# Attention and a maxout feed-forward layer: weight loads by column groups and six-tile groups of Q and K in place of whole-expert loads and per-tile loads, with another order

## The chip, the cores and the metric

The kernel runs on one core of a Trainium2 chip. The core has five engines with a queue each: TensorE (PE; its weight loads are listed as PEld), VectorE (DVE), ScalarE (ACT), GpSimd (POOL) and SyncE (SP), which here issues nearly all DMA transfers. The metric is the device time of one execution in microseconds (us). The kernel before took 182.6, 183.34 and 183.36 us in three runs; the median is 183.34 us.

## The reference

Input are q, k and v of four batches, eight heads, 768 positions and 64 elements a head, in fp32, and four weight matrices. First comes attention with a window: a query sees the keys at most 95 positions behind it, and the first eight keys of its batch.

```python
scores = scale * np.matmul(q, k.transpose(0, 1, 3, 2))
rel = pos[:, None] - pos[None, :]
is_global = pos[None, :] < int(n_global)             # 8
is_local = (rel >= 0) & (rel < int(n_local))         # 96
keep = is_global | is_local
dist = np.where(is_global & ~is_local, float(n_local), np.abs(rel))
scores = scores - slopes[:, None, None] * dist       # one slope a head
scores = np.where(keep, scores, -1000000000.0)
a = softmax(scores)
x = (a @ v), heads put side by side                  # 3072 x 512
```

Then comes a feed-forward layer with three experts, of which the largest value counts:

```python
h = np.maximum(np.maximum(x @ w1, x @ w2), x @ w3)   # 3072 x 768
return (h @ w_out).astype(np.float32)                # 3072 x 512
```

## The kernel before, in words

The 3072 positions are 24 tiles of 128, six to a batch. The whole program is one list of units, SCHEDULE (lines 25 to 57), written out by a planner and executed from left to right (lines 474 and 475). A unit is a letter and numbers; each issues its instructions to the engines' queues, and each engine works through its queue in this order. Waits between engines follow from the data and from the buffers. The letters (line 471):

- `l n.s` loads part s of group n of Q or K (line 151), `c n.s.how` casts it to bf16 (line 178), and `x n.s.how` transposes it on TensorE and copies it from PSUM to the transposed Q and K of the batch, qkT (line 226). A group is several tiles of a batch (GROUPS, line 91: first tile and number). A row of the load holds as many positions of a head as the group has tiles, so it is 256 bytes times that number. Groups of 2 tiles have two parts (Q and K, all heads), groups of 4 four parts, groups of 6 eight parts (two heads each).
- `L T` loads one tile of Q and K in rows of 256 bytes (line 160), `C T.0.how` casts it and `X T.how` transposes it, on TensorE or, with how 4, by a DMA transpose from SP's queue (line 245). `v T` loads V and `C T.1.how` casts it.
- `S T.g.how` computes the scores of four heads of a tile (g is 0 or 1) and their exponential on ACT (line 268). With how 1 TensorE adds the bias with two further matmuls; with how 0 a later unit `M T.g` multiplies by a mask on VectorE (line 302). `B` and `K` prepare the biases and masks.
- `A T.how` is the product with V and the division by the sum (line 311; how names which of two PSUM buffers it takes). `G` and `V` put the first eight keys and values of the batch into the tile, in place of its own (lines 209 and 218), once the tile's own are no longer needed.
- `T T.how` transposes the attention's result, on TensorE or (how 4) by DMA (line 335), into xT of a chunk. There are seven chunks, of 4, 2, 2, 4, 4, 4 and 4 tiles.
- `w g.j` loads weights of expert j (line 412), `W g.j.how` casts column group g of expert j (256 of 768 columns; line 425), `o` and `Q` do the same for w_out.
- `F c.f.j` computes 128 hidden columns f of chunk c for expert j with four matmuls (line 355). Expert 0's result is copied by ACT to a buffer h01, and VectorE takes the maximum with the other two.
- `O c.t.how` is one tile of the output: six matmuls, a copy and a store (line 385); `E` does the last chunk's (line 390).

In casts and copies how is 0 for ACT, 1 for VectorE and 2 for POOL. For `x`, how 0 and 1 transpose into the single PSUM buffer psT and copy on ACT and VectorE, 2 and 3 do so in the three buffers psH, which the `F` and `O` units use too, and 4 splits the copy between ACT and VectorE.

Buffers that matter: raw (6) for loads of Q and K, cast_pool (5), h01 (6), psH (3), psT (1), the two score buffers of PSUM sp0 and sp1 (1 each), and three stages for weights of 1.5 MB (line 414).

Of the kernel before, what the change touches and what calls it, by code (L numbers as in the profile page):

```python
# [12 lines left out]
FP32 = mybir.dt.float32  # L13
# [9 lines left out]


SCHEDULE = """
    B0.1 B1.1 B2.1 B3.1 v0 B4.2 l1.0 l1.1 K0 K1 K2 K3 K4 K5 K6 K7 B5.0 c0.0.2 c0.1.1 B6.1 x0.0.2 B7.1
    x0.1.4 v1 S0.0.1 S0.1.1 G0.2 S1.0.1 c1.0.2 x1.0.3 v2 M0.0 M0.1 S1.1.1 M1.0 C0.1.2 M1.1 A0.0 c1.1.2
    C1.1.2 l2.0 l2.1 x1.1.4 C2.1.0 A1.1 V1.1 c2.0.1 G1.0 T0.1 S2.0.1 T1.1 S2.1.0 G2.2 S3.0.1 S3.1.1 G3.0
    M2.0 M2.1 v3 C3.1.1 w0.0 M3.0 M3.1 A2.0 w0.1 v4 v5 w0.2 x2.0.2 l3.0 l3.2 V2.2 A3.1 T2.1 c2.1.2
    x2.1.4 T3.0 W0.0.1 S4.0.0 S4.1.1 F0.0.0 G4.2 S5.0.0 S5.1.0 W1.0.2 V3.1 F0.1.0 F0.2.0 W2.0.2 F0.3.0  # L30
    F0.4.0 F0.5.0 W1.1.0 l3.1 l3.3 M4.0 M4.1 W2.1.0 W0.2.2 v6 v7 C4.1.1 W0.1.1 M5.0 M5.1 C5.1.0 W1.2.0
    c3.0.2 A4.1 c3.2.2 F0.0.1 F0.1.1 F0.2.1 V4.1 F0.3.1 F0.4.1 F0.5.1 c3.1.2 c3.3.2 A5.0 T4.0 F0.0.2
    x3.0.2 W2.2.0 o2 o1 F0.1.2 F0.2.2 Q1.2 l4.0 T5.1 o0 x3.2.2 F0.3.2 x3.1.1 F1.0.0 F1.1.0 C6.1.1 x3.3.2
    F1.2.0 F0.4.2 S6.0.0 S6.1.0 G6.0 M6.0 M6.1 F0.5.2 S7.0.0 S7.1.0 G7.2 l4.1 F1.0.1 F1.0.2 F1.1.1
    F1.1.2 F1.3.0 A6.1 F1.2.1 F1.3.1 S8.0.0 S8.1.0 F1.2.2 F1.3.2 Q2.2 c4.0.2 C7.1.2 M7.0 M7.1 F1.4.0
    G8.2 F1.5.0 S9.0.0 S9.1.0 G9.2 F1.4.1 F1.5.1 F1.4.2 M8.0 v8 L12 L13 v9 Q0.0 c4.1.2 F1.5.2 v10 A7.0
    C8.1.0 x4.0.4 x4.1.2 O0.0.0 T6.0 M8.1 M9.0 V7.2 C12.0.1 O0.1.0 S10.0.0 L14 S10.1.0 G10.2 v11 M9.1
    M10.0 O0.2.1 X12.4 T7.1 O0.3.1 A8.0 C13.0.0 C9.1.0 V8.2 T8.4 F2.0.0 F2.1.0 F2.2.0 A9.1 X13.1 V9.2
    C14.0.0 v12 C10.1.2 F2.0.1 F2.1.1 F2.2.1 S11.0.0 S11.1.0 F2.3.0 F2.4.0 M10.1 M11.0 O1.0.0 X14.0
    M11.1 A10.1 V10.2 F2.0.2 F2.1.2 F2.2.2 T9.1 C11.1.0 S12.0.0 S12.1.0 G12.0 F2.3.1 F2.4.1 S13.0.0  # L40
    S13.1.0 F2.3.2 T10.0 F2.5.0 F2.4.2 A11.0 G13.2 M12.0 L15 L16 v13 v14 O1.1.1 F2.5.1 C12.1.0 T11.0
    S14.0.0 S14.1.0 G14.2 F2.5.2 M12.1 M13.0 M13.1 M14.0 M14.1 C13.1.1 C15.0.2 F3.0.0 F3.1.0 F3.2.0
    X15.4 C16.0.1 X16.4 A12.1 T12.4 F3.3.0 F3.4.0 v15 A13.0 L17 L18 v16 L19 F3.0.1 F3.1.1 F3.2.1 S15.0.0
    S15.1.0 G15.2 M15.0 O2.0.0 M15.1 F3.0.2 F3.1.2 C14.1.0 V13.2 A14.1 O2.1.0 S16.0.0 M16.0 S16.1.0
    G16.1 F3.3.1 F3.2.2 F3.3.2 C15.1.2 C17.0.0 V14.2 A15.1 T13.4 T14.4 T15.4 C18.0.2 X17.0 F3.4.1 F3.5.0
    V15.2 M16.1 C16.1.1 C19.0.2 S17.0.0 S17.1.0 F3.4.2 F3.5.1 F3.5.2 A16.0 X18.4 V16.2 v17 v18 M17.0
    X19.1 O3.0.0 O3.1.0 O3.2.0 C17.1.2 F4.0.0 F4.0.1 S18.0.0 S18.1.0 F4.0.2 G18.0 F4.1.0 v19 S19.0.0
    S19.1.0 F4.2.0 F4.3.0 L20 C20.0.2 T16.4 G19.1 M17.1 L21 M18.0 M18.1 M19.0 C18.1.2 F4.4.0 F4.1.1
    F4.5.0 M19.1 F4.2.1 F4.3.1 X20.4 A17.1 F4.1.2 C19.1.1 F4.4.1 F4.5.1 A18.0 A19.1 F4.2.2 F4.3.2 F4.4.2
    T17.4 S20.0.0 S20.1.0 F4.5.2 T18.4 T19.4 L22 O3.3.1 F5.0.0 C21.0.1 X21.4 C22.0.0 G20.2 F5.0.1 M20.0  # L50
    M20.1 F5.1.0 F5.2.0 X22.4 F5.1.1 F5.3.0 F5.4.0 S21.0.0 S21.1.0 F5.2.1 F5.3.1 F5.4.1 M21.0 G21.0
    S22.0.0 v20 L23 v21 v22 S22.1.0 F5.0.2 M21.1 M22.0 F5.5.0 F5.5.1 M22.1 C20.1.2 V19.2 A20.0 V20.2
    F5.1.2 F5.2.2 F5.3.2 C21.1.0 v23 A21.0 C23.0.0 X23.4 T20.4 T21.4 O4.0.1 V21.2 C22.1.2 A22.1 C23.1.1
    V22.2 O4.1.1 G22.2 F5.4.2 T22.4 S23.0.0 M23.0 S23.1.0 F5.5.2 O4.2.0 O4.3.0 M23.1 A23.1 T23.4 O5.0.1
    O5.1.1 O5.2.0 O5.3.0 F6.0.0 F6.1.0 F6.2.0 F6.0.1 F6.1.1 F6.3.0 F6.2.1 F6.3.1 F6.4.0 F6.0.2 F6.1.2
    F6.2.2 F6.5.0 F6.4.1 F6.3.2 F6.4.2 F6.5.1 F6.5.2 E
"""


# [1 line left out]
def kernel(  # L61
# [13 lines left out]
    nc = tc.nc  # L75
# [8 lines left out]
    DM = H * D  # L84
    DFF = moe_w1.shape[1]
# [2 lines left out]
    slopes = [2.0 ** (-8.0 * (h + 1) / H) for h in range(H)]  # L88
    sizes = [4, 2, 2, 4, 4, 4, 4]

    GROUPS = [[0, 2], [2, 2], [4, 2], [6, 4], [10, 2]]
    assert sum(sizes) == NTT
    chunks, where = [], {}
    for n in sizes:
# [15 lines left out]
    xT_pool = ctx.enter_context(tc.tile_pool(name="xT", bufs=3))  # L110
    stage_pool = ctx.enter_context(tc.tile_pool(name="stage", bufs=3))
    ht_pool = ctx.enter_context(tc.tile_pool(name="ht", bufs=2))
    h01_pool = ctx.enter_context(tc.tile_pool(name="h01", bufs=6))
    ost_pool = ctx.enter_context(tc.tile_pool(name="ost", bufs=4))
    psS = ctx.enter_context(tc.tile_pool(name="psS", bufs=1, space=bass.MemoryType.PSUM))
    psH = ctx.enter_context(tc.tile_pool(name="psH", bufs=3, space=bass.MemoryType.PSUM))
# [14 lines left out]
    w123 = [persist.tile([128, 4, 3, 256], BF16, name=f"w123_{i}") for i in range(3)]  # L131
# [12 lines left out]
    def part(n, s):  # L144

        T0, sz = GROUPS[n]
        jn = {2: 4, 4: 2, 6: 1}[sz]
# [3 lines left out]
    def load_part(n, s):  # L151

        bb, t0, sz, a, j0, jn = part(n, s)
        r = raw_pool.tile([128, 2 * DM], FP32, name="rawp", tag="raw")
        r = r[:, 0:sz * jn * 128].rearrange("i (h x) -> i h x", h=2 * jn)
        raw["p", n, s] = r
        src = (q, k)[a][bb, 2 * j0:2 * (j0 + jn), t0 * 128:(t0 + sz) * 128, :]
        nc.sync.dma_start(out=r, in_=src.rearrange("h (i e) d -> i h (e d)", e=sz))  # L158
# [17 lines left out]
    copies = (nc.scalar.copy, nc.vector.tensor_copy, nc.gpsimd.tensor_copy)  # L176
# [231 lines left out]
    wsrc = [moe_w1, moe_w2, moe_w3]  # L408

    wst = {}  # L410

    def load_w(g, j):

        st = stage_pool.tile([128, 4, DFF], FP32, name="wst", tag="wst")
        wst[j] = st
        nc.sync.dma_start(out=st, in_=wsrc[j].rearrange("(i p) f -> p i f", p=128))

    def load_wo(i):
        st = stage_pool.tile([128, 4, DFF], FP32, name="wost", tag="wst")
        st = st.rearrange("p i f -> p (i f)")[:, 0:2 * DM].rearrange("p (i f) -> p i f", i=2)  # L420
        wst["o", i] = st
        nc.sync.dma_start(out=st, in_=moe_w_out[i * 256:(i + 1) * 256, :].rearrange(
            "(i p) f -> p i f", p=128))

    def cast_w(g, j, how):
        copies[how](w123[g][:, :, j], wst[j][:, :, 256 * g:256 * (g + 1)])  # L426

    def cast_wo(i, how):
        copies[how](wo[:, 2 * i:2 * i + 2], wst["o", i])
# [7 lines left out]
    with tc.manual_schedule():  # L437
        load_part(0, 0)
        load_part(0, {2: 1, 4: 2, 6: 4}[GROUPS[0][1]])

# [6 lines left out]
        for tvar in va_ring + va_first:  # L447
# [21 lines left out]
        nc.vector.tensor_scalar_min(rbase[0:NG, 2, :], rbase[0:NG, 2, :], float(NL))  # L469

        units = {"l": load_part, "v": load_v, "c": cast_part, "x": u_x, "L": load, "w": load_w, "o": load_wo, "C": cast, "X": u_X, "S": u_S, "M": u_M,
                 "A": u_A, "G": put_kg, "V": put_vg, "T": u_XT, "F": u_F1, "W": cast_w,
                 "K": u_K, "B": u_B, "Q": cast_wo, "O": u_F2, "E": u_E, "D": u_D}
        for u in SCHEDULE.split():
# [34 lines left out]
```

The softmax here doesn't subtract the row's maximum and nothing guards it: scores larger than these inputs give would overflow.

## Time and profile before

The profiled execution took 182.6 us, and the profile's span is 180.8 us; the rest lies around it.

| engine | busy us | share of the span | instructions |
|---|---|---|---|
| PE | 166.4 | 92% | 1532 |
| PEld | 95.1 | 53% | 1552 |
| DVE | 119.1 | 66% | 233 |
| ACT | 104.5 | 58% | 159 |
| POOL | 38.0 | 21% | 66 |

The page divides the span in 40 slices of 4.52 us and gives each engine's busy share in tenths. A chain of waits is followed back from the last instruction; each line of it has a start, a duration and the work ("PE h L361 x47": 47 matmuls of line 361 in a row; "SPq": SP issuing a DMA; "DMA wst": a transfer). A timeline has start, duration, engine, line, operation and, in brackets, the idle time ahead of it and what ended it. A group has its count, busy time and mean duration. The time to landing of a DMA counts from its issue on SP. DMA queue q1, which SP's transfers use, moved 35.2 MB.

### The profile page before, as it was taken

The page shows a single profiled execution, that of the slowest core. Times are in us where ns is not written, and L with a number is a line of the kernel's source. Part 1 is how long each engine was busy: PE and PEld are TensorE (multiplying, and loading weights), DVE is VectorE, ACT ScalarE, POOL GpSimd, SP SyncE. Part 2 cuts the span into 40 slices and gives each one's busy share as a digit, 9 for nine tenths or more (in the row PEclk, how much of TensorE's full clock was granted, in tenths as well). Part 3 has the DMA queues.
Part 4 walks back from the last instruction along what each step waited for, and adds up shares of the span by engine and source line. Part 5 has one row for each costly group of instructions (what it writes and reads, how often), then busy time and mean ns, then how long its engine had stood idle before and what let it go on. Part 6 is the DMA issues. An engine that isn't in the chain of part 4 may idle for free.

```text
span 180.8 us, 3975 instructions
## 1 busy us (share of the span) xinstructions
PE 166.4 (92%) x1532; PEld 95.1 (53%) x1552; DVE 119.1 (66%) x233; ACT 104.5 (58%) x159; POOL 38.0 (21%) x66
## 2 busy tenths in 40 slices
PE   0598879999999999999999999999999999999990
PEld 0344635466777587755455544554445545444450
DVE  4538755986789787689758816597739984046600
ACT  4958878756779868974656358304566242421141
POOL 6470370261551020020123310400004300000000
PEclk9999999999999999999999999999999999999997
DMA  5999999999979798975599999925899664600024
GB/s 145 271 252 282 387 359 247 378 316 322 321 169 219 202 184 238 225 196 93 124 220 252 151 264 248 154 58 110 186 153 218 126 167 151 232 0 4 0 79 155
DMA packets 82035, 35.52 MB, mean 196 GB/s; under 512 B 66144, under 2 KB 76768, under 8 KB 82016
## 3 DMA queue, kind: packets, MB, share of 16 engines
q1 hardware_dynamic: 81872, 35.20, 84.5%
q8 instruction: 12, 0.20, 0.5%
q10 hardware_dynamic: 144, 0.07, 0.1%
q14 instruction: 7, 0.06, 0.1%
HBM read 25.17 MB, written 6.29 MB: 174 GB/s over the span
## 4 chain that ended last, share of the span: by engine, by line
PE 82%; SPq 7%; DMA 7%; issue 1%; ACT 1%; DVE 0%; ACTq 0%
PE h L361 52%; PE po L376 16%; DMA wst<-in_moe_w_dram 6%; PE sp L283 5%; SPq L158 4%; SPq L174 3%; PE op L322 3%; PE op L325 2%; PE tpp L239 1%; DMA out_dram<-ost 1%; PE tp L261 1%; PE xtp L349 1%; DVE w L426 0%; ACT P L288 0%; ACT ost L382 0%
## 5 line engine op out<-in xcount | busy, mean ns | idle before, releaser
L361 PE MATMUL h<-xT,w 128*128 128x512 bf16 (+1 forms) x491 | 99.0, 348 | 1.9 <-DVE w L426 1.1
L361 PEld LDWEIGHTS <-w 128*128 128x128 bf16 x504 | 46.9, 98 | 41.8 <-DVE w L426 1.3
L288 ACT ACTIVATE P<-sp 128x1024 bf16<-128x1024 f32 (+1 forms) x48 | 43.4, 953 | 24.2 <-PE sp L283 24.2
L368 DVE TENSOR_TENSOR h<-h,h 128x512 bf16<-128x512 bf16 (+1 forms) x42 | 25.1, 608 | 20.3 <-PE h L361 17.1
L376 PE MATMUL po<-wo,ht 128*128 128x512 bf16 (+2 forms) x149 | 33.2, 362 | 0.4
L366 ACT CAST h<-h 128x512 bf16<-128x512 f32 (+1 forms) x42 | 21.4, 533 | 17.7 <-PE h L361 17.4
L370 DVE TENSOR_TENSOR ht<-h,h 128x512 bf16<-128x512 bf16 (+1 forms) x42 | 24.9, 608 | 8.7 <-PE h L361 8.0
L307 DVE TENSOR_TENSOR P<-P,wmask 128x1024 bf16<-128x1024 bf16 x34 | 22.9, 693 | 5.1 <-ACT P L288 5.1
L376 PEld LDWEIGHTS <-ht 128*128 128x128 bf16 x156 | 14.2, 98 | 14.0
L382 ACT COPY ost<-po 128x512 f32<-128x512 f32 (+2 forms) x17 | 9.3, 556 | 20.5 <-PE po L376 19.0
L332 DVE TENSOR_TENSOR xb<-op,rz 128x512 bf16<-128x512 f32 x24 | 16.6, 691 | 0.8
L283 PEld LDWEIGHTS <-qkT 64*128 64x128 bf16 x352 | 10.1, 95 | 10.9 <-issue 8.0
L283 PE MATMUL sp<-qkT 64*128 64x128 bf16 x352 | 15.5, 221 | 0.1
L239 PE MATMUL tpp<-identb,qkp 128*128 128x128 bf16 x96 | 8.0, 234 | 6.7 <-POOL qkp L183 6.4
L322 PEld LDWEIGHTS <-P 128*128 128x128 bf16 x192 | 12.5, 97 | 2.8 <-ACT P L288 0.5
L322 PE MATMUL op<-va,P 128*128 128x65 bf16 x160 | 12.5, 193 | 0.6 <-ACT P L288 0.6
L325 PEld LDWEIGHTS <-P 128*128 128x128 bf16 x160 | 10.4, 97 | 1.7 <-issue 0.2
L183 POOL CAST qkp<-rawp 128x1024 bf16<-128x1024 f32 x10 | 10.5, 1052 | 2.3 <-DMA rawp<-in_k_dram 1.2
L239 PEld LDWEIGHTS <-qkp 128*128 128x128 bf16 x96 | 6.4, 105 | 7.8 <-POOL qkp L183 6.7
L382 DVE COPY ost<-po 128x512 f32<-128x512 f32 (+1 forms) x9 | 5.8, 643 | 6.4 <-PE po L376 6.4
L325 PE MATMUL op<-va,P 128*128 128x65 bf16 x128 | 9.9, 193 | 0.1
L221 POOL COPY va<-vaf 8x260 int32<-8x260 int32 x13 | 5.6, 430 | 20.5 <-PE op L325 14.5
(64 smaller groups left out, 111.7 us busy)
## 6 DMA issues: line engine op xcount, KB each, us to landing
rawv<-in_v_dram SPq DMA_DIRECT2D x24, 256.0 KB, 5.2
out_dram<-ost SPq DMA_DIRECT2D x23, 256.0 KB, 2.3
wst<-in_moe_w_dram SPq DMA_DIRECT2D x3, 1536.0 KB, 10.3
rawp<-in_q_dram SPq DMA_DIRECT2D x6, 512.0 KB, 7.3
rawp<-in_k_dram SPq DMA_DIRECT2D x6, 512.0 KB, 7.9
raw<-in_q_dram SPq DMA_DIRECT2D x12, 256.0 KB, 4.9
raw<-in_k_dram SPq DMA_DIRECT2D x12, 256.0 KB, 5.1
wost<-in_moe_w_out_dram SPq DMA_DIRECT2D x3, 512.0 KB, 6.9
```

Source lines behind the costliest of these rows:

```text
L239: nc.tensor.transpose(tp[:, e, j - lo], qb["p", n, s][:, e, 2 * j:2 * j + 2].rearrange("i h d -> i (h d)"), identb)
L283: nc.tensor.matmul(sp[:, hh, j2, ds], qT(T - ds, 1)[hsl, jp], qT(T, 0)[hsl, jp], start=not how, stop=True, skip_group_check=True)
L288: nc.scalar.activation(P[:, :, 0:n], sp.rearrange("p a b d n -> p (a b) d n")[:, :, 0:n], AF.Exp, bias=0.0, scale=scale)
L307: nc.vector.tensor_mul(P, P, wmask[:, g, :, 0:2])
L322: nc.tensor.matmul(o, P[:, i, 0], heads(va[T])[:, h], start=True, stop=(t == 0), skip_group_check=True)
L325: nc.tensor.matmul(o, P[:, i, 1], heads(va[T - 1])[:, h], start=False, stop=True, skip_group_check=True)
L332: nc.vector.tensor_tensor(out=x.rearrange("p (g h) d -> p g h d", g=2), in0=o4[:, :, :, 0:64], in1=rz[:, :, :, None].to_broadcast([128, 2, ...
L361: nc.tensor.matmul(ps, w123[f // 2][:, dm, j, (f % 2) * 128:(f % 2) * 128 + 128], xT[c][:, dm], start=(dm == 0), stop=(dm == 3))
L366: nc.scalar.copy(h01, ps)
L368: nc.vector.tensor_max(h01s[c, f], h01s[c, f], ps)
L370: nc.vector.tensor_max(ht[c][:, f], h01s[c, f], ps)
L376: nc.tensor.matmul(po, ht[c][:, f, tt * 128:(tt + 1) * 128], wo[:, f, cols], start=(f == 0), stop=(f == NF - 1))
```

## The change

There are four parts.

1. GROUPS: the fourth group is tiles 6 to 11 (all of batch 1) in place of tiles 6 to 9, the fifth is tiles 12 to 17 (all of batch 2) in place of tiles 10 and 11. Both have eight parts of 128 rows for two heads, 1536 bytes a row. Tiles 12 to 17 have no `L`, `C T.0` and `X` units any longer; tiles 18 to 23 keep them.
2. Each expert's weights come in two loads: columns 0 to 255 (0.5 MB, rows of 1024 bytes; `w0.j`) and columns 256 to 767 (1 MB, rows of 2048 bytes; `w1.j`). They have stages of their own, three each; w_out takes the first kind.
3. h01 has four buffers in place of six.
4. The list is planned anew.

```diff
-    GROUPS = [[0, 2], [2, 2], [4, 2], [6, 4], [10, 2]]
+    GROUPS = [[0, 2], [2, 2], [4, 2], [6, 6], [12, 6]]
...
-    h01_pool = ctx.enter_context(tc.tile_pool(name="h01", bufs=6))
+    h01_pool = ctx.enter_context(tc.tile_pool(name="h01", bufs=4))
...
     def load_w(g, j):
-        st = stage_pool.tile([128, 4, DFF], FP32, name="wst", tag="wst")
-        wst[j] = st
-        nc.sync.dma_start(out=st, in_=wsrc[j].rearrange("(i p) f -> p i f", p=128))
+        n = 256 * (1 + g)
+        st = stage_pool.tile([128, 4, n], FP32, name="wst", tag=f"wst{g}")
+        wst[g, j] = st
+        nc.sync.dma_start(out=st, in_=wsrc[j][:, 256 * g:256 * g + n].rearrange("(i p) f -> p i f", p=128))
 
     def load_wo(i):
-        st = stage_pool.tile([128, 4, DFF], FP32, name="wost", tag="wst")
-        st = st.rearrange("p i f -> p (i f)")[:, 0:2 * DM].rearrange("p (i f) -> p i f", i=2)
+        st = stage_pool.tile([128, 2, DM], FP32, name="wost", tag="wst0")
...
     def cast_w(g, j, how):
-        copies[how](w123[g][:, :, j], wst[j][:, :, 256 * g:256 * (g + 1)])
+        src = wst[0, j] if g == 0 else wst[1, j][:, :, 256 * (g - 1):256 * g]
+        copies[how](w123[g][:, :, j], src)
```

Of the list, the beginning up to the first hidden units and the stretches that the prediction names:

```diff
-    B0.1 B1.1 B2.1 B3.1 v0 B4.2 l1.0 l1.1 K0 K1 K2 K3 K4 K5 K6 K7 B5.0 c0.0.2 c0.1.1 B6.1 x0.0.2 B7.1
-    x0.1.4 v1 S0.0.1 S0.1.1 G0.2 S1.0.1 c1.0.2 x1.0.3 v2 M0.0 M0.1 S1.1.1 M1.0 C0.1.2 M1.1 A0.0 c1.1.2
-    C1.1.2 l2.0 l2.1 x1.1.4 C2.1.0 A1.1 V1.1 c2.0.1 G1.0 T0.1 S2.0.1 T1.1 S2.1.0 G2.2 S3.0.1 S3.1.1 G3.0
-    M2.0 M2.1 v3 C3.1.1 w0.0 M3.0 M3.1 A2.0 w0.1 v4 v5 w0.2 x2.0.2 l3.0 l3.2 V2.2 A3.1 T2.1 c2.1.2
-    x2.1.4 T3.0 W0.0.1 S4.0.0 S4.1.1 F0.0.0 G4.2 S5.0.0 S5.1.0 W1.0.2 V3.1 F0.1.0 F0.2.0 W2.0.2 F0.3.0
+    K0 K1 l1.0 l1.1 B0.1 B1.1 B2.2 B3.1 B4.0 B5.0 B6.1 c0.0.0 B7.1 c0.1.1 c1.0.2 x0.0.3 K2 K3 K4 x0.1.4
+    S0.0.1 S0.1.1 G0.0 x1.0.3 c1.1.2 K5 K6 S1.0.1 S1.1.1 v0 v1 x1.1.2 K7 C0.1.1 G1.2 C1.1.1 M0.0 M0.1
+    A0.0 M1.0 M1.1 A1.1 S2.0.1 T0.1 v2 C2.1.1 S2.1.1 G2.2 V1.1 l2.0 v3 M2.0 C3.1.2 T1.1 c2.0.1 l2.1
+    S3.0.0 S3.1.1 G3.0 M2.1 M3.0 A2.0 V2.2 c2.1.2 w0.0 W0.0.2 x2.0.2 M3.1 A3.1 w0.1 T2.0 x2.1.4 T3.0
+    S4.0.0 S4.1.0 M4.0 G4.0 W0.1.2 w0.2 F0.0.0 F0.1.0 w1.0 W1.0.2 W0.2.0 W2.0.0 V3.1 v4 F0.0.1 S5.0.0
+    S5.1.0 F0.1.1 F0.0.2 F0.1.2 F0.2.0 F0.3.0 M4.1 M5.0 w1.1 M5.1 C4.1.2 A4.1 F0.4.0 F0.5.0 W2.1.1 V4.1
+    W1.1.2 T4.0 F0.2.1 w1.2 W1.2.0 F0.3.1 F0.4.1 l3.0 W2.2.1 v5 l3.4 l3.1 l3.5 C5.1.2 l3.2 F0.5.1 c3.0.0
+    c3.4.2 F0.2.2 x3.0.2 l3.6 A5.0 l3.3 F0.3.2 F0.4.2 l3.7 o1 o2 x3.4.2 c3.1.2 o0 T5.1 c3.5.0 F0.5.2 v6
+    c3.2.2 c3.6.2 F1.0.0 x3.1.3 v7 x3.5.0 l4.0 c3.3.2 v8 v9 F1.0.1 F1.1.0 F1.1.1 Q1.2 x3.2.1 F1.2.0
+    F1.3.0 x3.6.2 c3.7.1 l4.4 F1.2.1 x3.3.3 x3.7.0 F1.0.2 F1.1.2 S6.0.0 M6.0 S6.1.0 F1.3.1 F1.4.0 G6.0
...
+    c4.1.2 c4.5.2 x4.4.2 O1.0.0 M9.0 M9.1 M10.0 A8.0 F2.0.0 F2.1.0 T8.4 V8.2 x4.1.2 x4.5.0 F2.0.1 c4.2.2
...
+    x4.2.2 c4.3.1 c4.7.2 M11.1 A10.0 F2.3.0 F2.4.0 C11.1.1 x4.6.2 x4.3.2 F2.1.2 V10.2 A11.1 T10.4 T11.4
+    x4.7.0 F2.2.2 F2.3.1 S12.0.0 S12.1.0 M12.0 F2.3.2 F2.5.0 G12.1 S13.0.0 S13.1.0 G13.2 F2.4.1 L18
+    F2.5.1 F2.4.2 F2.5.2 S14.0.0 S14.1.0 F3.0.0 M12.1 v12 v13 M13.0 M13.1 C18.0.2 F3.0.1 v14 F3.1.0
+    F3.2.0 v15 v16 F3.3.0 M14.0 C12.1.1 A12.1 C13.1.0 G14.1 C14.1.2 M14.1 O2.0.0 A13.1 F3.1.1 V13.2 L19
```

In the list before, chunk 3's last token transposes are `T9.1`, `T10.0` and `T11.0` on TensorE, and tiles 13, 14, 17 and 19 have their Q and K transposed on TensorE (`X13.1`, `X14.0`, `X17.0`, `X19.1`), the other tiles from 12 on by DMA.

More of the change, by code (lines that the diff above doesn't have):

```diff
@@ L31 @@
[L31 to L55, printed above, removed]
@@ L56 @@
-    F6.2.2 F6.5.0 F6.4.1 F6.3.2 F6.4.2 F6.5.1 F6.5.2 E
+    K0 K1 l1.0 l1.1 B0.1 B1.1 B2.2 B3.1 B4.0 B5.0 B6.1 c0.0.0 B7.1 c0.1.1 c1.0.2 x0.0.3 K2 K3 K4 x0.1.4
[3 more added lines that the diff above has]
+    S4.0.0 S4.1.0 M4.0 G4.0 W0.1.2 w0.2 F0.0.0 F0.1.0 w1.0 W1.0.2 W0.2.0 W2.0.0 V3.1 v4 F0.0.1 S5.0.0
@@ new lines @@
+    S7.0.0 S7.1.0 Q2.1 F1.2.2 l4.1 l4.5 F1.4.1 F1.3.2 C6.1.1 F1.4.2 G7.2 S8.0.0 S8.1.0 Q0.2 G8.2 O0.0.0
+    C7.1.1 O0.1.0 F1.5.0 c4.0.0 c4.4.2 l4.2 l4.6 v10 M6.1 M7.0 M7.1 M8.0 M8.1 A6.0 A7.1 V7.2 l4.3 l4.7
+    C8.1.0 O0.2.0 x4.0.3 F1.5.1 S9.0.0 v11 C9.1.2 S9.1.0 T6.1 O0.3.0 F1.5.2 G9.2 S10.0.0 S10.1.0 T7.1
+    c4.1.2 c4.5.2 x4.4.2 O1.0.0 M9.0 M9.1 M10.0 A8.0 F2.0.0 F2.1.0 T8.4 V8.2 x4.1.2 x4.5.0 F2.0.1 c4.2.2
+    c4.6.2 A9.0 F2.2.0 F2.0.2 M10.1 G10.0 F2.1.1 S11.0.0 T9.4 S11.1.0 C10.1.2 F2.2.1 M11.0 V9.2 O1.1.0
@@ new lines @@
+    x4.2.2 c4.3.1 c4.7.2 M11.1 A10.0 F2.3.0 F2.4.0 C11.1.1 x4.6.2 x4.3.2 F2.1.2 V10.2 A11.1 T10.4 T11.4
+    x4.7.0 F2.2.2 F2.3.1 S12.0.0 S12.1.0 M12.0 F2.3.2 F2.5.0 G12.1 S13.0.0 S13.1.0 G13.2 F2.4.1 L18
+    F2.5.1 F2.4.2 F2.5.2 S14.0.0 S14.1.0 F3.0.0 M12.1 v12 v13 M13.0 M13.1 C18.0.2 F3.0.1 v14 F3.1.0
+    F3.2.0 v15 v16 F3.3.0 M14.0 C12.1.1 A12.1 C13.1.0 G14.1 C14.1.2 M14.1 O2.0.0 A13.1 F3.1.1 V13.2 L19
+    T12.4 F3.0.2 A14.0 F3.2.1 F3.1.2 T13.4 S15.0.0 S15.1.0 G15.2 v17 V14.2 M15.0 F3.3.1 C15.1.0 C16.1.1
@@ new lines @@
+    L20 C19.0.2 F3.2.2 M15.1 F3.3.2 S16.0.0 S16.1.0 M16.0 G16.0 F3.4.0 F3.5.0 A15.0 V15.1 X18.4 M16.1
+    F3.4.1 T14.4 T15.4 F3.4.2 O2.1.1 S17.0.0 M17.0 S17.1.0 X19.4 F3.5.1 F3.5.2 S18.0.0 M17.1 M18.0
+    S18.1.0 G18.1 F4.0.0 F4.1.0 v18 C20.0.3 A16.1 v19 F4.2.0 T16.4 V16.1 L21 M18.1 F4.3.0 S19.0.0 L22
+    S19.1.0 C21.0.2 C17.1.1 G19.2 X20.4 F4.0.1 F4.1.1 M19.0 F4.2.1 F4.0.2 F4.4.0 F4.1.2 M19.1 C18.1.2
+    X21.4 F4.5.0 F4.3.1 C22.0.2 L23 C23.0.2 C19.1.0 F4.2.2 A17.0 F4.3.2 A18.1 O3.0.1 O3.1.1 v20 v21
@@ new lines @@
+    S20.0.0 T17.4 S20.1.0 F4.4.1 O3.2.0 G20.0 T18.4 A19.0 T19.4 F4.4.2 F4.5.1 F4.5.2 S21.0.0 S21.1.0
+    X22.4 O3.3.0 O4.0.0 V19.2 M20.0 C20.1.1 X23.4 O4.1.0 C21.1.2 M20.1 A20.1 V20.1 F5.0.0 F5.1.0 F5.2.0
+    G21.2 S22.0.0 S22.1.0 M21.0 M21.1 v22 v23 T20.4 F5.0.1 F5.1.1 M22.0 F5.3.0 F5.0.2 F5.1.2 C22.1.1
+    A21.0 T21.4 G22.0 V21.1 F5.2.1 F5.3.1 M22.1 S23.0.0 M23.0 C23.1.0 S23.1.0 M23.1 F5.4.0 O4.2.0 F5.4.1
+    A22.1 T22.4 V22.2 F5.2.2 A23.0 F5.3.2 T23.4 F5.5.0 F5.4.2 F5.5.1 F5.5.2 O4.3.0 F6.0.0 F6.1.0 F6.2.0
@@ L57 @@
+    F6.0.1 F6.1.1 F6.2.1 O5.0.1 O5.1.0 F6.3.0 F6.0.2 F6.1.2 F6.2.2 F6.4.0 O5.2.1 O5.3.1 F6.5.0 F6.3.1
+    F6.4.1 F6.3.2 F6.4.2 F6.5.1 F6.5.2 E
 """
```

## The prediction

> **What bounds the kernel now.** I read the page's head and slices first, then the chain of waits in order of time, the TensorE timeline around its biggest step, and the groups by shape, for prices.
>
> ```profile
> span 180.8 us, 3975 instructions
> PE 166.4 (92%) x1532; PEld 95.1 (53%) x1552; DVE 119.1 (66%) x233; ACT 104.5 (58%) x159; POOL 38.0 (21%) x66
> PE   0598879999999999999999999999999999999990
> ```
>
> TensorE is full from slice 6 (22.6 us) on. The lead-in is what isn't. The chain says what fills it:
>
> ```profile
> 11.35 1.04 SPq L158
> ...
> 12.43 1.51 SPq L174
> ...
> 13.99 9.97 DMA wst<-in_moe_w_dram
> 23.98 0.71 DVE w L426
> ...
> 24.73 0.39 PE h L361
> ...
> 155.98 10.14 PE h L361 x47
> ...
> 171.52 3.49 PE po L376 x17
> ```
>
> To 24.73 us the end hangs on the loads and on the first 1.5 MB of weights; after that on TensorE alone. The timeline shows what TensorE had ready while it waited:
>
> ```profile
> 21.94 0.40 PE L349 MATMUL xtp<-identb,xb 128*128 128x128 bf16 x4
> ...
> 22.70 0.60 PE L275 MATMUL sp<-bias,identb 128*128 128x512 bf16 x2
> 23.24 0.40 PE L283 MATMUL sp<-qkT 64*128 64x128 bf16 x8
> 24.73 1.04 PE L361 MATMUL h<-xT,w 128*128 128x512 bf16 x3 [1.10 <-DVE w L426]
> ```
>
> The tokens of tile 3 were transposed at 21.94, tile 4's scores ended at 23.64, and only 1.10 us was pure waiting for weights. So earlier weights alone are worth 1.1 us; more needs an earlier token chain too.
>
> How dense is the rest? Prices from the chain's pieces: 47 matmuls of 512 columns in 10.14 us, 0.216 each; 12 of 256 in 1.31, 0.109; a pair of score groups 0.55 (0.33 at a batch's first tile); an A unit 0.47 (0.26); eight transposes 0.445, 0.0555 each. From F0.0.0 on: 90 hidden units of four tiles (0.864) and 36 of two (0.434) 93.4; 20 output units of 1.294, 25.9; scores 9.8; A 8.8; 108 transposes 6.0; the last block 5.2. Sum 149.1. Up to F6.0.0 it is 128.4, which put on 24.73 gives 153.1; the chain has F6.0.0 at 155.98. So before loses only 2.9 us to small waits. The order after can gain at the start, and lose anywhere.
>
> **What the skill says.** "DMA: Bandwidth & Descriptors", Specifications, wants at least 512 B per transfer for line rate. The trace agrees, and goes further. By the landings: v (256 KB, rows of 256 B) 1.1 us behind the load before it; a part of 512 KB in 512 B rows 1.8; one in 1024 B rows 1.5; a 1.5 MB weight load in 3072 B rows 5.2, 4.1 and 4.3. "Perfetto Trace Analysis", DVE / Act Engine Instruction and its neighbours, calls ACT, DVE and GPSIMD strict FIFO; here every queue runs in schedule order, so a cast that waits for a load holds all behind it. "GPSIMD Engine Reference", Specifications, says its SBUF interfaces are shared with VectorE; the trace has POOL's 1024-element weight cast at 1.04 to 1.70 us, so I keep both ends.
>
> **The change, part by part.**
>
> *First weights.* The same loads stand before w0.0 in either order (six parts, four v's), so the last of them lands near 18.75 in both. w0.0 is now 0.5 MB in 1024 B rows: 1.5, and up to 1.1 more (what the first weight load took over the second): 20.25 to 21.35. Its cast moves from VectorE (0.69) to POOL, behind V2.2 (0.40) and c2.1.2 (1.03). Ready at 21.3 to 23.0.
>
> *Token chain.* K0 and K1 go first, ACT casts c0.0, VectorE copies x0.0. The first scores stay near 9.0: they wait for c0.1 (6.85) as now. Then x1.1 is copied on ACT after S1's exponentials, which I put at 11.6 and 12.6 (now 11.83 and 13.15). S2's exponentials (0.97 each) start near 15.05 (now 15.91). S3.0 and S4.1 lose their bias matmuls (before S2.1 keeps one), two fewer in all here: one group less, 0.43. Counting on: S2 to 17.0, S3 to 19.0, A3 19.05 to 19.5, its VectorE pair 0.9, T3's transposes and ACT copy to 21.8. Upper bound: before's 23.64 less the 0.43 of bias, 23.2. F0.0.0 also stands behind S4.1. So F0.0.0 starts between 21.9 and 23.2; I take 22.5, as casts and copies are in step there. Gain 2.2 us.
>
> *Weights behind it.* w0.1 and w0.2 land 1.5 apart, w1.0 (1 MB) about 2.75 later (two thirds of 4.1): 26.0 to 27.0. W2.0.0 sits on ACT ahead of S5's exponentials: cast 1.0, two exponentials 1.95, so A4.1 can start at 29 to 30. TensorE reaches A4.1 7.5 us after F0.0.0, at 30.0; F0.2.0, behind W1.0.2 on POOL, at 28.2 against 27.0 to 28.7 (my central values: 29.5 and 27.8). Just covered. If w1.0 lands after 27.2, every us late is paid. W2.1.1 and W1.2.0, waiting on w1.1 and w1.2, have over 0.5 us of cover.
>
> *Groups of six.* Batches 1 and 2 load K and Q whole: 16 loads of 0.38 MB in place of four parts of 1024 B rows, two of 512 B, and 12 loads of 256 B rows (tiles 12 to 17). Queue time: 12×1.1+4×1.5+2×1.8 = 22.8 goes, 16×1.1 = 17.6 comes (0.38 MB at the 1024 B rate). TensorE doesn't wait for the queue there, so no gain counted. SP's issues: 18 become 16, weights 3 become 6, at 0.4 to 1.8 each. S6 now needs all 3.1 MB of batch 1: v4, w1.1, w1.2 and v5 take the queue to about 34.8, the eight l3 loads to about 42.2. S6 comes near 46.7. Covered by 4 us. o0 lands near 46.5, its cast ends by 48, O0.0.0 comes at 50.8.
>
> *TensorE's transposes.* 48 more in parts, 32 fewer of single tiles, 12 fewer of tokens (T9, T10, T11 go to DMA): +4, 0.22 us.
>
> *Copies and casts.* Sixteen part copies of 768 elements: between ACT's rows of 0.59 (512) and 1.01 (1024), 0.80; VectorE 0.68 and 1.22, 0.95. ACT has twelve, 9.6 us for 6.7 before; three token copies go (two ACT ones, 1.2), casts on ACT shrink by 0.6. ACT +1.1 us from F0 to F3. POOL has 11 casts of about 0.83 for seven of 1.04: +1.8, with 4 us of slack on S6. One mask multiply (0.69) comes on VectorE under S3.0.
>
> *Moved DMA transposes.* T10.4 and T11.4 now lead to F3.0.0: xb11 near 72.2, SP issue 1.2, landing 2.4 to 5.0 after issue start, 74.6 to 77.2 against F3.0.0 at 76.4: 0 to 0.8, mostly 0. Behind T11.4 on SP stand L18 (two issues, 0.6 each) and v12, issued near 74.8; at 3.4 to 5.2 it lands by 80.0, cast 0.4, A12 at 80.7. T12 to T23 have 1.5 us or more. h01's four buffers: every F x.y.0 stands behind the last use four back; zero, else one VectorE step of 0.68.
>
> Sum against the profiled execution (182.6; span 180.8): -2.2 +0.2 +0.4 (waits above what before has: half of T11's 0.8) = -1.6, 181.0. The median shown is 0.74 over the profiled one: **181.7 us**.
>
> **The rivals.**
> 1. *Start half won* (0.20). The token chain keeps before's pace (23.2), or w1.0 lands at 28: gain 1.1 to 1.5, less 0.2 and 0.4 and another 0.5 of waits: 182.4 to 184.2, no change. For: margins at A4.1 and F0.2.0 are below 1 us. Against: the queue before showed no such delay except at the first weight load, and I have that in my upper end.
> 2. *ACT-evacuated parts block the hidden ring* (0.34, slower). Eleven of the sixteen parts take a buffer of psH, three deep, shared with the hidden units; ACT empties eight of them (x3.0, x3.4, x3.6, x4.1, x4.2, x4.3, x4.4, x4.6). If one lands behind two exponentials (1.95), the other two buffers cover two units of two tiles, 0.87: 1.1 us each. The start gain of 2.0 is gone after two, and slower by 0.9 from three on: 184.6 with three, 185.7 with four. For: ACT is at 5.3 to 5.6 of 6 us from 54 to 66 already. Against: in this order x3.6, x4.2, x4.6 and x4.3 don't follow exponentials directly; x4.4 does, but with O1.0 (1.3) after it.
> 3. *DMA time bounds the middle* (inside rival 1). Freed queue time would then show as gain, 1 us: 180.7. Against: no TensorE wait names a load after 24.73.
>
> **How the numbers follow.** Forecast 0.46, rival 1 0.20, rival 2 0.34. About 0.5% (0.9 us) is what a measurement can tell from none. Of the forecast's 0.46 all but 0.02 lies below 182.4; rival 1 gives 0.02 of faster: faster 0.46, same 0.20, slower 0.34. Low end: start 2.8 and no extra waits, 180.5. The high end reaches into rival 2 between three and four blocked parts, 185.3; above it some 0.12, below 180.5 some 0.07. The forecast's own range is 180.5 to 182.4.
>
> **What would show it.** F0.0.0 at 22.5 (right if 21.9 to 23.2) and F6.0.0 near 154.4. w0.0 landing before 21.4; w1.0 before 27.2; no TensorE wait on ACT P before A4.1. S6 not waiting on a load. If F6.0.0 less F0.0.0 exceeds 132.5 us (before 131.25), rival 2 or an unseen wait is at work, and the gaps before units with psH show which. If F0.0.0 stays above 23.2, the token step is wrong.

## The result and the profile after

The changed kernel takes 180.56 us (median; 180.48 to 180.85) against 183.23 us before (the median with a fourth execution): a ratio of 0.9864, 95% interval 0.9838 to 0.989. The forecast was 181.7 us, with 180.5 to 185.3 as its range; the result lies 0.06 us above the range's low end. The profiled executions are 182.6 us (span 180.8) and 180.48 us (span 178.7), so 2.1 us of span are to be found. The medians differ by 2.67 us; nearly all of the 0.6 us between these two figures lies in executions of the kernel before that have no trace.

The page of the changed kernel, head and TensorE's slices:

```profile
span 178.7 us, 3987 instructions
PE 165.4 (93%) x1534; PEld 95.2 (53%) x1554; DVE 121.3 (68%) x240; ACT 103.0 (58%) x160; POOL 38.4 (22%) x65
PE   0598799999999999999999999999999999999991
```

TensorE works as long as before, within 1 us; it is full one slice sooner. Its chain of waits (start, duration, work) reads differently at the front:

```profile
12.37 7.86 DMA rawp<-in_k_dram
20.22 0.05 issue
20.27 1.05 POOL qkp L184
21.32 0.04 issue
21.37 0.41 PE tpp L240 x4
21.80 0.59 ACT qkT L244
22.40 0.05 issue
22.44 0.73 PE sp L284 x16
23.17 0.32 PE h L362
...
149.07 1.08 PE h L362 x5
...
169.79 1.94 PE po L377 x9
...
175.63 0.27 ACT ost L383
```

The first hidden unit starts at 23.17 in place of 24.73, 1.56 us sooner. What releases it is no longer a weight: it stands behind the scores of tile 4, and these behind l2.1, the last part of Q and K ahead of the weights (the DMA of the first line). From the first hidden unit to the last output block are 169.79 - 23.17 = 146.62 us; before it was 171.52 - 24.73 = 146.79. From there to the end of the span are 8.9 us, before 9.3. So of 2.1 us, 1.56 are the start, 0.17 the long middle, and some 0.37 lie at the very end: from the end of the chain's last copy, at 175.90 (before 177.61), to the end of the span it is 2.8 us, before 3.2. No change was aimed at that stretch, and its cause stays open.

TensorE's waits on other engines in the changed kernel (who for whom, us in total, times, longest):

```profile
PE tpp L240 <- ACT qkp L184: 6.5, 1, 6.5
PE tpp L240 <- POOL qkp L184: 0.8, 1, 0.8
PE sp L276 <- ACT P L289: 0.5, 1, 0.5
PE op L323 <- ACT P L289: 0.4, 1, 0.4
```

Two more of 0.2 us are left out. All of them come before 23 us. The 0.8 is l2.1's cast; before, the corresponding line was 1.1 us for the weights' cast. No entry stands for a weight, and none for a part of six.

### The profile page after: what moved, and what is told of

The parts are those of the page before. It is cut to its first block, busy times and chain, and to the rows that moved or that the text cites. A ratio compares the mean times of both kernels' runs of the same rounds, so it can differ in the third digit from the quotient of the medians.

```text
span 178.7 us, 3987 instructions
## 1 busy us (share of the span) xinstructions
PE 165.4 (93%) x1534; PEld 95.2 (53%) x1554; DVE 121.3 (68%) x240; ACT 103.0 (58%) x160; POOL 38.4 (22%) x65
## 4 chain that ended last, share of the span: by engine, by line
PE 83%; SPq 6%; DMA 6%; issue 1%; ACT 1%; POOL 1%; ACTq 0%
PE h L362 53%; PE po L377 16%; PE sp L284 6%; DMA rawp<-in_k_dram 4%; SPq L175 3%; PE tpp L240 3%; SPq L159 3%; PE op L323 3%; PE op L326 2%; DMA out_dram<-ost 1%; PE xtp L350 1%; ACT ost L383 1%; POOL qkp L184 1%; ACT qkT L244 0%; ACTq L383 0%
## 5 line engine op out<-in xcount | busy, mean ns | idle before, releaser
L362 PE MATMUL h<-xT,w 128*128 128x512 bf16 (+1 forms) x489 | 100.1, 348 | 0.7
L362 PEld LDWEIGHTS <-w 128*128 128x128 bf16 x504 | 46.7, 98 | 40.2
L367 ACT CAST h<-h 128x512 bf16<-128x512 f32 (+1 forms) x42 | 21.9, 527 | 20.8 <-PE h L362 20.2
L371 DVE TENSOR_TENSOR ht<-h,h 128x512 bf16<-128x512 bf16 (+1 forms) x42 | 25.4, 608 | 8.7 <-PE h L362 7.9
L308 DVE TENSOR_TENSOR P<-P,wmask 128x1024 bf16<-128x1024 bf16 x35 | 24.0, 709 | 3.6 <-ACT P L289 3.6
L383 ACT COPY ost<-po 128x512 f32<-128x512 f32 (+2 forms) x19 | 10.6, 562 | 19.6 <-PE po L377 17.9
L240 PE MATMUL tpp<-identb,qkp 128*128 128x128 bf16 x144 | 12.0, 233 | 7.3 <-ACT qkp L184 6.5
L244 ACT COPY qkT<-tpp 128x768 bf16<-128x768 bf16 (+2 forms) x16 | 12.6, 801 | 5.4 <-PE tpp L240 5.3
L240 PEld LDWEIGHTS <-qkp 128*128 128x128 bf16 x144 | 9.9, 104 | 9.0 <-ACT qkp L184 6.5
L184 POOL CAST qkp<-rawp 128x768 bf16<-128x768 f32 (+1 forms) x14 | 12.2, 878 | 11.2 <-DMA rawp<-in_k_dram 6.0
L199 POOL CAST qkb<-raw 128x1024 bf16<-128x1024 f32 x5 | 5.2, 1040 | 22.3 <-DMA raw<-in_k_dram 22.3
```

Source lines behind the costliest of these rows:

```text
L240: nc.tensor.transpose(tp[:, e, j - lo], qb["p", n, s][:, e, 2 * j:2 * j + 2].rearrange("i h d -> i (h d)"), identb)
L308: nc.vector.tensor_mul(P, P, wmask[:, g, :, 0:2])
L362: nc.tensor.matmul(ps, w123[f // 2][:, dm, j, (f % 2) * 128:(f % 2) * 128 + 128], xT[c][:, dm], start=(dm == 0), stop=(dm == 3))
L367: nc.scalar.copy(h01, ps)
L371: nc.vector.tensor_max(ht[c][:, f], h01s[c, f], ps)
```

## The experiments

In what follows, waypoints are the starts of every 24th hidden matmul on TensorE (of its weight load), read from each trace, so that they can be compared where two orders have the same work ahead of them. "Landing" is a load's issue plus its time to landing. Each kernel was timed beside the kernel before, whose median was 182.83 to 183.23 us in these comparisons; a ratio is to that median. A trace shows one execution, the medians are over 2 to 20.

### Half of the change at a time

Three kernels cross the start with what follows. First the split of the weights alone, in the list before:

```diff
-    ... v3 C3.1.1 w0.0 M3.0 M3.1 A2.0 w0.1 v4 v5 w0.2 ...
+    ... v3 C3.1.1 w0.0 w1.0 M3.0 M3.1 A2.0 w0.1 w1.1 v4 v5 w0.2 w1.2 ...
```

> The kernel before with its weights split by columns and nothing else changed (0.5 MB and 1 MB of an expert directly behind each other, h01 and groups as before). Start theory (the gain is that F0.0.0 starts earlier; the order after it is worth nothing): the first weights stop being the last to come, F0.0.0 follows S4.1, which ended at 23.64, so it starts near 23.7 in place of 24.73: 182.2 us. Rival that the split alone is the whole gain: 180.6. Rival that the groups of six and the order behind F0.0.0 are the gain: 183.2.

Measured: 182.84 us, ratio 0.9988 (0.9968 to 1.0008), no change. F0.0.0 started at 24.25, only 0.48 sooner. Its waits on TensorE, and F0.0.0 in its chain, say why:

```profile
PE op L323 <- DVE va L190: 1.4, 1, 1.4
...
24.25 0.97 PE h L362 x4
```

A3 waited 1.4 us for the cast of v3, which landed at 19.83; in the kernel before v3 landed at 18.74. w0.0 landed at 21.31 in place of 23.95, as wanted. The split brought the weights forward and the load just ahead of them back. The half us that was gained stayed to the end: the last waypoint is at 165.5 against 166.0. So the split alone is not the gain.

Second, the old list up to F0.0.0 (without its early v4, v5 and parts of batch 1), then the new list with groups of six:

```diff
-    (the changed list up to F0.0.0)
+    B0.1 B1.1 B2.1 B3.1 v0 B4.2 l1.0 l1.1 K0 ... v3 C3.1.1 w0.0 M3.0 M3.1 A2.0 w0.1 w0.2 x2.0.2 V2.2 A3.1
+    T2.1 c2.1.2 x2.1.4 T3.0 W0.0.1 S4.0.0 S4.1.1 F0.0.0
```

> The list of before up to F0.0.0, with split weights, then the changed kernel's list with its groups of six. Start theory: F0.0.0 near 23.7, 0.6 later than in the changed kernel, the rest alike: 181.1 us. Rival that groups of six and the order behind are worth most: as the changed kernel, 180.6. Rival that the rest depends on the lead (casts on POOL and ACT come late for it): above 181.6.

Measured: 181.11 us, ratio 0.9897 (0.9836 to 0.9957). In the traced execution F0.0.0 started at 23.37, 0.2 us later than in the changed kernel, and the last waypoint stayed 0.2 us behind (164.4 against 164.2):

```profile
23.37 2.69 PE h L363 x12
```

Here v3 landed at 18.71, and three small loads follow it, not a small and a large one. In this execution the old lead-in, with this order of loads, is nearly as early as the new one. But the traced execution (180.64 us) is one of the faster two of four; the others took 180.41, 181.57 and 182.55, where the changed kernel's four lie within 0.37 us. Where the slower two lost their time is in no trace, so the new lead-in may be worth more than 0.2.

Third, the new list up to F0.0.0, then the old list with its groups of four and single-tile loads:

```diff
-    (the old list up to F0.0.0) ... F0.0.0 G4.2 S5.0.0 S5.1.0 ...
+    (the changed list up to F0.0.0, with w0.0 w1.0 for its three small loads)
+    F0.0.0 w0.1 v4 v5 w1.1 w0.2 w1.2 l3.0 l3.2 S5.0.0 S5.1.0 ...
```

> The changed kernel's list up to F0.0.0, then the list of before with its groups of four and its single-tile loads, weights split. Start theory: F0.0.0 near 23.1 as in the changed kernel, the rest as dense as before: 181.6 us. Rival that groups of six and the order behind are worth most: not below 182.2, as with the split alone.

Measured: 182.42 us, ratio 0.9972 (0.9955 to 0.9988). F0.0.0 was early, its matmuls from 23.30, but the waypoint that before reached at 43.2 came at 43.6, and the last one at 166.1 (before 166.0): in the traced execution nothing was kept of the start. TensorE's waits, added to those of the lead-in:

```profile
PE sp L284 <- ACT qkT L217: 0.7, 1, 0.7
PE tpp L240 <- POOL qkp L184: 0.6, 1, 0.6
```

The first is the copy G4.0, which my join put on ACT behind two exponentials; that is the join's fault. The second is l3.0's cast: in the kernel before l3.0 landed at 35.90 and x3.0 ran at 37.98; here it landed at 37.04 and x3.0 had to wait for its cast, until 38.19. In the old order an earlier start runs into the loads of batch 1. To see whether that is the whole of it, both were mended:

```diff
-    F0.0.0 w0.1 v4 v5 w1.1 w0.2 w1.2 l3.0 l3.2
+    F0.0.0 w0.1 v4 w1.1 w0.2 v5 l3.0 w1.2 l3.2
...
-    G4.0
+    G4.2
```

> As the run with the new lead-in and the old order behind it, with two things mended that its trace names: the copy G4 goes to POOL as in the list before (on ACT it stood behind two exponentials), and l3.0 is loaded ahead of w1.2 (it landed at 37.04, 1.1 later than in the kernel before, while TensorE came earlier). Theory that the old order keeps an earlier start only as far as its loads come in time: F0.0.0 at 23.1 and x3.0 near 36.9 in place of 38.2, 181.8 us. Rival that the old order loses the start gain whatever is mended: 182.4 as that run.

Measured: 182.2 us, ratio 0.9951 (0.9934 to 0.9968), between the two. l3.0 landed at 34.02, so x3.0 was free; now the next part held. From this kernel's chain:

```profile
30.23 8.03 DMA rawp<-in_k_dram
38.30 0.08 issue
38.38 1.05 POOL qkp L184
39.43 0.05 issue
39.48 0.62 PE tpp L240 x8
```

This is l3.2, behind w1.2 in the queue. Of 1.5 us won at F0.0.0, 0.7 were left at the end (165.3 against 166.0). In these two runs each load put forward pushed another back, and the old order kept none and about half of the earlier start. What the changed kernel does at this point is in its own loads: l3.0, now 0.38 MB and ahead of v5, landed at 35.19, and its cast was on ACT, at once (35.21).

Set side by side, all with split weights, and the new order always with its groups of six: old lead-in and old order 182.84 us, new lead-in and old order 182.42 (182.2 mended), old lead-in and new order 181.11, both new 180.56. The time is won at the start, but it is the order of the loads and of what follows F0.0.0 that keeps it. The theory of the first run, that "the order after it is worth nothing", was wrong.

### The new order with the old loads

The changed kernel with each expert's weights in one load again:

```diff
-    n = 256 * (1 + g) ... wst[g, j]
+    st = stage_pool.tile([128, 4, DFF], FP32, name="wst", tag="wst") ... wst[j]
-    w1.0 ... w1.1 ... w1.2
```

> The changed kernel with each expert's weights in one load of 1.5 MB again, order otherwise as changed. Start theory: w0.0 lands near 24.0, POOL's cast ends at 25.0, so F0.0.0 comes at 25.0; w0.1 lands near 28.0 and w0.2 near 32.4, so F0.0.2 can start near 33.5 in place of 27.3: TensorE loses about 6 us there, 186.5 us. Rival that only the first load counts (later ones hidden): 1.9 us lost, 182.5.

Measured: 187.22 us, ratio 1.022 (1.0162 to 1.0278). F0.0.0 came at 25.20, and TensorE waited for weights three times:

```profile
PE h L363 <- POOL w L428: 2.8, 2, 2.5
PE h L363 <- ACT w L428: 1.5, 1, 1.5
```

The loss is 6.7 us against the changed kernel, near what the landings gave (186.5 us expected; only two executions). The order, which asks for three experts' first columns ahead of any expert's others, and the split are one change; neither is to be had alone.

The groups, put back in the same manner: parts of four and two tiles and single-tile loads at the places of the parts of six, all transposed on TensorE.

```diff
-    GROUPS = [[0, 2], [2, 2], [4, 2], [6, 6], [12, 6]]
+    GROUPS = [[0, 2], [2, 2], [4, 2], [6, 4], [10, 2]]
-    l4.0 l4.4 l4.1 l4.5 l4.2 l4.6 ... x4.0.3 x4.4.2 x4.1.2 x4.5.0 x4.2.2 x4.6.2
+    L12 L13 L14 L15 L16 L17 ... X12.1 X13.0 X14.0 X15.0 X16.0 X17.0
```

> The changed kernel with the groups of before (four tiles, two tiles, then single-tile loads in 256 B rows for tiles 12 to 17), each put at the places of the parts of six, all of tiles 6 to 17 still transposed on TensorE (96 transposes in either). Theory that the groups are worth nothing in time (queue time in the middle is hidden, TensorE's work is equal): 180.6 us. Rival that rows of 1536 B and smaller parts are what the order behind F0.0.0 needs: 181.5 or more.

Measured: 183.45 us, ratio 1.0029 (1.0012 to 1.0045): the whole gain is gone, with F0.0.0 at 23.21. Its waypoints fall behind the changed kernel's: 41.7 against 41.3, 46.6 against 45.4, 65.0 against 63.2, 70.9 against 67.6. Who waited for whom in the stretch from 40 to 76 us:

```profile
POOL qkb L199 <- DMA raw<-in_k_dram: 11.4, 5, 6.4
...
PE tp L262 <- ACT qkT L267: 1.1, 1, 1.1
```

and of its chain there:

```profile
64.64 5.65 DMA raw<-in_k_dram
70.33 0.08 issue
70.41 0.92 POOL qkb L199
71.33 0.55 issue
71.88 0.61 POOL va L190
72.50 0.81 POOL va L222
73.31 0.04 issue
73.35 0.19 PE op L326
```

L17's second half landed at 70.29; POOL's cast of it stands ahead of a V cast and of V's global rows, and A waited for these. The single-tile transposes, which all go through the one buffer psT, waited another 1.1 us for ACT's copy out of it (the line above) and 0.5 us for VectorE's. Each single-tile half (256 KB) landed 1.1 us behind the one before it, 2.2 us a tile; the changed kernel's parts (384 KB) landed 1.05 apart, 1.4 us a tile. So the groups do matter to this order, and the rival of this run's expectation came true. This run changes sizes and PSUM buffers as well as rows, and the share of each was not separated.

One more step, the six tiles by DMA transposes:

```diff
-    X12.1 X13.0 X14.0 X15.0 X16.0 X17.0
+    X12.4 X13.4 X14.4 X15.4 X16.4 X17.4
```

> As the run with the groups of before, but tiles 12 to 17 have their Q and K transposed by DMA: 48 transposes fewer on TensorE, 2.7 us at 0.0555, and six PSUM copies fewer. Theory that TensorE alone is the bound from F0.0.0 on: 178.0 us. Rival that six DMA transposes more, at 1.2 to 1.9 us of SP each, make token transposes and stores late: 180.6 or more.

Measured: 192.72 us, ratio 1.0535 (1.0504 to 1.0566). TensorE has less to do and waits more:

```profile
PE op L323 <- POOL va L190: 4.8, 2, 4.7
PE h L362 <- issue: 3.4, 1, 3.4
```

The first wait is not for SP's time alone. This kernel's list of all waits, and its chain from 69 us on, have these lines:

```profile
POOL qkb L199 <- DMA qkT<-qkb: 3.8, 1, 3.8
...
69.42 4.11 DMA qkT<-qkb
...
74.66 0.62 POOL va L190
```

X12.4 stood in SP's queue behind loads and a store; it was issued at 69.42, 12 us after tile 12's cast (57.17), and landed at 73.53. Until then it held one of the five cast buffers, POOL's cast of tile 17 waited for that buffer, the V cast of tile 10 behind it on POOL came at 74.66, and A10 waited 4.7 us. The second wait is F3.0.0's for the token transpose T11.4, issued at 85.80 behind X16.4, X17.4 and T10.4 and landed at 88.25. Behind both waits the granted TensorE clock was low, 0.53 from 76.0 to 79.6 us and 0.76 from 88 to 95: an estimated 3.4 us of TensorE's time, from these two figures. Why it was low is not known. Taking work from the busiest engine was no gain here, where it went to a queue, and held buffers, that others waited for.

### The late landing ahead of the weights

In the changed kernel l2.1 landed at 20.22, 3.3 us behind v3 at 16.93, where 1.8 had been counted. Is it this load, or its place as the last small load ahead of the weights?

```diff
-    ... l2.0 v3 M2.0 C3.1.2 T1.1 c2.0.1 l2.1 ...
+    ... l2.0 l2.1 v3 M2.0 C3.1.2 T1.1 c2.0.1 ...
```

> The changed kernel with the load l2.1 ahead of v3. In the changed kernel l2.1 landed 3.3 us after v3, in place of the 1.8 counted. Theory that the lateness belongs to the last small load ahead of the weights: v3 lands near 20.2, its cast ends near 20.9 on POOL and A3 (19.7 now) comes near 21.3, so F0.0.0 near 24.0: 181.5 us. Rival that it belongs to l2.1: it lands by 18, F0.0.0 comes at 22.9, behind its weights' cast: 180.4.

Measured: 181.26 us, ratio 0.9908 (0.9874 to 0.9942). l2.1 landed at 18.05, v3 at 20.18, F0.0.0 started at 24.0, and TensorE had a new wait:

```profile
PE op L324 <- POOL va L191: 1.2, 1, 1.2
```

In the traced execution it was the place, by the numbers expected. But the six executions fall in two groups, 180.40, 180.49 and 180.66 us and 181.85, 181.93 and 181.96, and the traced one is of the slower: half of them took the time that the rival named. So this run does not decide. Traces of one order differ too. The run with the six DMA transposes has the changed kernel's loads up to w1.2, and in it l2.1 landed at 18.91 and w0.0 took 2.9 us for its usual 1.5; the two runs with the new lead-in ahead of the old order have the same loads up to w1.0, and the first had it on w0.0 (l2.1 at 18.73), the second on l2.1 (20.31). The extra, 1.0 to 1.5 us, was paid once in each of the twelve traces, by the last small load or by the first weights behind it (in the kernel before by the first weights, 5.2 us for 4.1). Which of the two pays is not set by the order alone; what sets it was not settled.

### Two prices

The rival that parts of six block the PSUM ring of the hidden units, priced by putting two of them behind a pair of exponentials:

```diff
-    ... S11.1.0 C10.1.2 F2.2.1 ... O1.1.0 x4.2.2 ... C11.1.1 x4.6.2 x4.3.2 ...
+    ... S11.1.0 x4.2.2 x4.6.2 C10.1.2 F2.2.1 ... O1.1.0 ... C11.1.1 x4.3.2 ...
```

> The changed kernel with the parts x4.2 and x4.6 moved to right behind S11's scores, so that two buffers of psH are held until ACT has done two exponentials. Prediction's rival 2 prices a part held so at 1.1 us: with two of three buffers held 1.1 to 2.2 us slower, 181.7 to 182.8. If the units around it cover the wait: 180.6.

Measured: 181.19 us, ratio 0.9908 (0.9885 to 0.9931), 0.6 us above the changed kernel's median; its fastest execution, 181.15, lies above the changed kernel's slowest, 180.85. Its trace from 60 to 80 us has one wait of TensorE on another engine:

```profile
PE po L378 <- DVE h L370: 0.6, 1, 0.6
```

From F0.0.0 to the last output block the two traces differ by 0.9 us. So two parts, held on purpose, cost 0.6 to 0.9 us together: less than expected for a block, and not fully covered either. The price of 1.1 each was too high by a factor of two or more.

And the buffers of h01:

```diff
-    h01_pool = ctx.enter_context(tc.tile_pool(name="h01", bufs=4))
+    h01_pool = ctx.enter_context(tc.tile_pool(name="h01", bufs=6))
```

> The changed kernel with six h01 buffers in place of four. Theory that four are enough in this order (each copy stands behind the last use four back): 180.6 us. Rival that the fourth buffer makes ACT wait for VectorE: up to 1 us faster, 179.6.

Measured: 180.48 us, ratio 0.9849 (0.9786 to 0.9911), as the changed kernel. Its F0.0.0 started at 22.7, though nothing ahead of it differs; with the same lead-in the other runs have 22.9 to 23.2. That is the scatter of the start from execution to execution, so a difference of 0.3 us in F0.0.0 between two traces shows nothing.

## Why the prediction was right, and where not

*What bounds the kernel, the start.* Right: F0.0.0 was put between 21.9 and 23.2 and came at 23.17, and 1.56 of the 2.1 us of span are there. The 22.5 taken was 0.7 too early. The step that was mis-sized is the landing of the loads: "the last of them lands near 18.75 in both", where l2.1 came at 20.22, and "up to 1.1 more" for w0.0, which came at 21.73, 0.4 past the upper end. In each trace with split weights either w0.0 or the load just ahead of it took 1.0 to 1.5 us more than its like, and w0.0 landed at 21.3 to 21.8. In the changed kernel l2.1's own route, cast, transposes, copy and scores, released F0.0.0, with the weights' cast (ended at 22.82) and tile 3's tokens (copy ended near 22.9) 0.2 to 0.3 us ahead of it. That l2.1 was late cost little: in the trace of the six DMA transposes, with the same lead-in, it landed at 18.91, and the weights released F0.0.0 only 0.2 us sooner:

```profile
14.03 7.79 DMA wst<-in_moe_w_dram
...
21.88 1.05 POOL w L428
...
22.98 2.76 PE h L362 x12
```

A small misreading stands at the front: slice 6 of the page before (from 22.6 us) is at 7 tenths; TensorE is full from the next one, at 27.1. The timeline on which the argument rests shows the wait all the same.

*The token chain.* The walk held to 0.1 to 0.7 us (S1's exponentials 11.74 on for 11.6, S2's 15.38 for 15.05, A3 19.74 for 19.05), and tile 3's tokens, counted to 21.8, were copied near 22.9. But "more needs an earlier token chain too" credited the new lead-in with too much, as far as the traces go: the old one, with the three small loads, starts F0.0.0 at 23.37. Between these two traces the new lead-in is worth 0.2 us, within the scatter, and the weights nearly all; by the medians, 181.11 and 180.56, it may be worth half a us.

*Weights behind it.* w1.0 landed at 27.54, half a us past the upper end, and ACT idled 0.71 us for it. A4.1 started at 30.68 and TensorE did not wait, because F0.0.0 was late by as much. W1.0's cast ended at 28.63 and F0.2.0 started at 28.7: "just covered", to within 0.1 us. Rival 1 was near.

*Groups of six.* The loads were 1.4 us later than counted and S6 0.9 (l3's from 35.19 to 43.58 for 42.2, S6 at 47.57 for 46.7), so the cover of 4 us was there and nothing waited. The sum held too: the middle takes as long as before. But the reason given, that queue time doesn't matter there since TensorE never waited, was wrong as a general step. It held for these two orders, each with its own loads. With the old groups in the new order the kernel loses 2.9 us, all of it behind F0.0.0, and with the old order behind a start 1.5 us earlier half of that start or all of it is lost, on l3.2 and l3.0. So the queue was close behind TensorE, in the former run up to 70 us; the waits of the profile before do not show it, since there the loads came in time (l3.0's cast ended at 36.99 for x3.0 at 37.98).

*Copies, casts, transposes.* Rival 2 is refuted by the changed kernel's trace (no such wait) and its price by the run that held two parts. T11.4 was issued at 74.44 and landed at 76.88, F3.0.0 came at 78.3: covered, so the 0.4 of added waits wasn't needed.

*The sum.* -2.2 +0.2 +0.4 was -1.6 of span; measured -2.1: -1.56 at the start, -0.17 in the middle with the 0.2 of transposes in it, -0.37 at the end, for which nothing was counted. So the gain at the start was forecast 0.6 too high, and that the sums agree to half a us is in part luck: 0.4 of waits that did not come, 0.37 at the end that was not foreseen, and a middle 0.17 shorter where 0.2 longer was counted. The last step added the 0.74 us between the profiled execution of before and its median, to 181.7; the changed kernel's profiled execution is within 0.1 us of its median, and the one of before was the fastest of its runs. This step is over half of the 1.1 us by which the forecast lay too high; the medians moved by 2.7 for 1.6 forecast.

*A check that was badly put.* "F6.0.0 less F0.0.0 exceeds 132.5" compared unlike stretches. The new list moves the four output units of chunk 5 behind F6.0.0 (5.2 us): 125.9 us were measured. The stretch to the last output block is the one that has the same work.

## What to carry to other kernels

When a chain shows the first weights as the last to arrive, split them by what is used first and plan the order anew for that: here the same split in the old order gained nothing measurable, and the new order with whole loads lost 2% against the kernel before. An order can fit its loads closely (here F0.2.0 came 0.1 us behind W1.0's cast); before giving a start gain as kept, look up for each of the next loads when it landed and when it was used. Look at the single times of a run, not only at its median: where they fall in two groups, one trace shows only one of them. And an engine's idle list is no measure of the queue behind it: read the distance between landing and use.

## What was not expected of the hardware

Where the queue passes from loads of rows of 256 and 512 B to weights of 1024 B and more, one load took 1.0 to 1.5 us longer than its like, in each of the twelve traces. It is now the last small load (l2.1 at 20.22 for 18.7, v3 at 20.18 with the two exchanged), now the first weights (5.2 us for 4.1 before, 2.9 for 1.5 with the old lead-in), and with one and the same order of loads it was either. That the row lengths are the cause is not shown. Two more measured surprises: six more DMA transposes cost 9 us over the same kernel with them on TensorE (192.72 against 183.45), far above their issue times of 1.2 to 1.9 us each, by a held buffer, late tokens and a lower granted clock; and with nothing changed ahead of it, F0.0.0 moves by 0.5 us from one trace to another (22.7 to 23.2).
